# Sinkhorn attention and token/channel MLP on one core: first k mixing, q turns, k row tiles and the bf16 copies of u rearranged

## The chip, the core and the metric

The kernel runs on one core of one Trainium2 chip. The core has a matrix engine (TensorE, PE in the profile, with its weight loads as PEld), a vector engine (DVE), a scalar engine (ACT), GpSimd (POOL) and a sync engine (SP, which here only issues transfers); each takes its instructions in order. Matrix products read SBUF and write PSUM, which has eight banks; DVE and ACT bring results from PSUM to SBUF. The metric is the device time of one execution in microseconds (us).

## The reference, cut to what matters

```python
P = sort_net                                   # (4, 8, 8, 8): batch, head, block, block
for _ in range(5):
    P = exp(P - max(P, -1)); P /= sum(P, -1) + 1e-9; P /= sum(P, -2) + 1e-9
k_sorted = einsum('bhij,bhjcd->bhicd', P, k in 8 blocks of 96 tokens)
v_sorted = einsum('bhij,bhjcd->bhicd', P, v in 8 blocks of 96 tokens)
attn = softmax(0.125 * q_block @ k_sorted_block.T)      # within each block
x    = (attn @ v_sorted), heads side by side            # (4, 768, 512)
u    = x + lam * (w_tok @ (alpha1 * x + beta1))         # token mixing, w_tok 768 x 768
out  = u + lam * (relu((alpha2 * u + beta2) @ w_ch1) @ w_ch2)   # 512 -> 2048 -> 512
```

q, k and v have four batches, eight heads, 768 tokens and 64 columns. Everything comes in and goes out as float32; the products are made in float16 and bfloat16.

## The kernel before, in words

**The front (batch 0).** The five rounds of the softmax on `sort_net` run on DVE and ACT (L223 to L238); between ACT's exponential and DVE's next step, a list of small set-up operations (`side`, L192) is worked off two at a time. PE meanwhile runs `dense(14)`, products with the identity that nobody reads. `big_p(b)` (L251) spreads the 8x8 matrices of a batch into `PB[b]`, a block matrix of 128 rows. `k_group(b, g)` (L303) mixes the blocks of k, 32 small products of 32 rows in PSUM tile `psA` (two banks; two such tiles), emptied half by ACT and half by DVE into `kT`; six groups make a batch. In a group before the change, the rows used are two of the four 32-row strips of PE. `q_pair(b, p, pool, eng)` (L290) turns q of two heads by 12 transposes into one bank, and `eng` copies it to `qT`; the bank is from `psX`, which has a single buffer, or from `psM`, which has three. `v_first_layout` (L141) rearranges batch 0's v, in four parts, on POOL and ACT; `v_first` (L323) mixes it in eight groups. Then `score` (scores, and their maxima on DVE), `split_max` and `turn_max` (the maxima turned), `soft` (scores again minus the maximum, exponential on ACT) and `value` (weighted sum of v on PE, normalised by DVE into `x16`) are written out by hand from L560 to L632, between `w_tok_block` (the turn of w_tok) and `row_sums`.

**The rest.** Three things are generators that yield a cost after each piece, and `weave(main, other, ratio)` (L548) puts pieces of `other` between those of `main` as long as their cost stays under `ratio` times the cost of `main` so far. It so fixes the order of the instructions on every engine:

- `opening()`: token mixing of batch 0 (`token_mix`, L470: six tiles of 128 tokens, each six products of 512 columns, two or three DVE operations and a bf16 copy `u16` by ACT, L486), with the first four `u_turn` (L488: u turned on PE, ACT makes `a2T` of it) after four tiles. Woven with `ahead(1)` (L453): mixing of batch 1's v (`v_group`, then `v_relay`, a trip through DRAM), four `q_pair` on `psX` with ACT, six `k_group`.
- `both()`: `hidden(b, 0)` (16 groups of four products with W1), three `result` (16 products with W2, two DVE operations, a write of 256 KB), `hidden(b, 1)`; woven with `attention(b + 1)` (L434).
- `join()`: token mixing of batch b+1 with the three other results of batch b; woven with `ahead(b + 2)`.

The last batch has hidden and result alone. The order of transfers is that of the queues: POOL issues the loads of q, k, v, w_tok, W1 and W2, SP the small vectors, the relay of v and the results.

Of the kernel before, what the change touches and what calls it, by code (L numbers as in the profile page):

```python
# [19 lines left out]
def kernel(  # L20
# [20 lines left out]
    BLK = S // NB  # L41
# [105 lines left out]
    v_first_layout(1, G)  # L147
    v_first_layout(3, G)
    load_k(1)
    load_q(1)  # L150
# [14 lines left out]
    V.memset(v0T[:, BLK * D:], 0.0)  # L165
    ones_bf = wt([128, 1], BF, "ones_bf")
# [21 lines left out]
    def products():  # L188
        for n in range(2):
# [3 lines left out]
        lambda: V.tensor_copy(ident16[:], ident32[:]),  # L193
# [9 lines left out]
        lambda: V.tensor_reduce(  # L203
            m32[:], ident32[:].rearrange("p (g c) -> p c g", c=32), AXX, ALU.add
        ),
        lambda: V.tensor_scalar(nmask[:], m32[:], -1.0, None, op0=ALU.mult),
        lambda: make_sel(1),
        products,
# [5 lines left out]
    warm = bank(psM)  # L214

    def dense(n):
        for _ in range(n):
            PE.matmul(
                warm[:], identbf[:], identbf[:].unsqueeze(1).to_broadcast([128, 4, 128]),
                start=True, stop=True,  # L220
            )
# [3 lines left out]
    for it in range(5):  # L225
        A.activation(sortP[:], sortP[:], AF.Exp)
        for _ in range(2):
            side.pop(0)()
# [10 lines left out]
    dense(14)  # L239
# [6 lines left out]
    for n in range(2):  # L246
        SP.dma_start(vecs[n].rearrange("(c p) -> c p", p=128), va[:, n])
    SP.dma_start(a2col[:], moe_alpha2.rearrange("(c p) -> p c", p=128))
    SP.dma_start(b2col[:], moe_beta2.rearrange("(c p) -> p c", p=128))

# [39 lines left out]
    def q_pair(b, p, pool, eng):  # L290
        ps = bank(pool, F16)
        for kt in range(NT):
# [6 lines left out]
            eng, qT[b % 2][p][:, 0:S].rearrange("r (t k) -> r t k", k=NT),  # L299
            ps[:, 0:S].rearrange("r (k t) -> r t k", k=NT),  # L300
        )

    def k_group(b, g):  # L303
        raw, ps = rawk[b % 2], bankA()
        for turn in range(2):
            for tt in range(8):
                for hl in range(2):
                    bk = (hl + turn) % 2
                    th, tl = divmod(g * 16 + bk * 8 + tt, HALF)
                    r = slice(th * 64 + hl * 32, th * 64 + hl * 32 + 32)  # L310
                    PE.matmul(  # L311
                        ps[hl * 64:hl * 64 + 64, bk, tt * 32:(tt + 1) * 32],
# [4 lines left out]
        dst = kT[:, 0:H4 * S].rearrange("r (c t) -> r c t", t=BLK)  # L317
        dst = dst[:, :, g * 16:(g + 1) * 16].rearrange("r c (b t) -> r c b t", b=2)
        src = ps[:, :, 0:256].rearrange("r b (t c) -> r c b t", c=32)
# [114 lines left out]
    def attention(b):  # L434
        for p in range(H4):
            for g in range(2):
                score(b, p, g)
            yield 0.65
# [14 lines left out]
    def ahead(b):  # L453
# [6 lines left out]
        for p in range(H4):  # L460
            q_pair(b, p, psX, A)
            yield 0.4
# [7 lines left out]
    def token_mix(b, kt):  # L470
# [15 lines left out]
        A.copy(u16[:, kt], ub[:, kt])  # L486

    def u_turn(b, half, ci):  # L488
        ps = bank(psM, BF)
# [31 lines left out]

    def result(b, half, kk, turn=None):
        kt = half * 3 + kk
        ub = u[b]
# [23 lines left out]
    def weave(main, other, ratio):  # L548
        done = given = 0.0
        live = True  # L550
        for cost in main:
            done += cost
            while live and given < ratio * done:
# [6 lines left out]
    big_p(0)  # L560
    V.memset(mh[0][:], 0.0)
    for n in range(2):
        V.memset(ET[n][:, :, :, BLK:], 0.0)
    k_group(0, 0)
    k_group(0, 1)
    q_pair(0, 0, psM, V)
    k_group(0, 2)
    dense(1)
    q_pair(0, 1, psX, V)
    k_group(0, 3)  # L570
    dense(1)
    q_pair(0, 2, psM, V)
    k_group(0, 4)
    dense(1)
    q_pair(0, 3, psX, V)
    k_group(0, 5)
    dense(2)
    v_first_layout(0, A)
    v_first_layout(2, A)
    for g in range(2):  # L580
        score(0, 0, g)
    dense(2)
    for g in range(2):
        score(0, 1, g)
    dense(3)
    split_max(0, 0, 2)
    score(0, 2, 0)
    w_tok_block(0, A)
    turn_max(0)
    score(0, 2, 1)  # L590
    w_tok_block(1, A)
    v_first(0, V)
    v_first(1, A)
    for g in range(2):
        soft(0, 0, g)
    v_first(2, A)
    v_first(3, V)
    for g in range(2):
        score(0, 3, g)
    v_first(4, A)  # L600
    v_first(5, V)
    split_max(0, 2, 4)
    w_tok_block(2, A)
    for g in range(2):
        soft(0, 1, g)
# [99 lines left out]
```

## Time and profile before

| what | value |
|---|---|
| median of 3 runs | 339.48 us (338.79 to 341.17) |
| the profiled execution, its own time | 339.23 us |
| its span, first to last instruction | 337.1 us |
| mean granted clock of PE | 0.931 |
| PE busy, DVE busy, ACT busy, POOL busy | 300.1, 181.9, 137.9, 28.7 us |
| first small k product, first score, first value | 13.51, 24.88, 37.26 us |
| first token mixing, first hidden product | 50.97, 81.00 us |
| joins of batches 1, 2, 3 begin | 123.65, 197.70, 268.62 us |
| last product ends, last write issued | 332.4, 333.9 us |

A row of the windows gives the stretch in us, its length, and for each engine its busy time and number of instructions, then the granted clock of PE (1.00 is full), the share of the 16 transfer engines and GB/s. A row of waits names who waited for whom, the sum, how often and the longest. A row of the timeline gives start, duration, engine, line, operation, output and inputs, and in brackets the idle time ahead of it and what ended it. A group row gives line, engine, operation, shapes and count, then busy time and the mean ns of one. L numbers are those of the listing above.

### The profile page before, as it was taken

How to read it: one execution, taken by the hardware profiler on the slowest of the kernel's cores; microseconds unless marked ns; L12 is line 12 of the kernel's file. 1: busy time of each engine (PE TensorE's matmuls, PEld its weight loads, DVE VectorE, ACT ScalarE, POOL GpSimd, SP SyncE). 2: the span in 40 equal slices, each digit the busy share in tenths (PEclk: the TensorE clock that was granted, in tenths of full speed). 3: DMA queues.
4: the chain of work that ended last, by engine and by line, in shares of the span. 5: the costliest groups of instructions: out<-in, count | busy, mean ns of one | idle time of the engine just before them, and what ended most of it. 6: DMA issues, size and time to landing. Idle time of an engine off the chain costs nothing.

```text
span 337.1 us, 7773 instructions
## 1 busy us (share of the span) xinstructions
PE 300.1 (89%) x3453; PEld 170.7 (51%) x3453; DVE 181.9 (54%) x345; ACT 137.9 (41%) x242; POOL 28.7 (9%) x45
## 2 busy tenths in 40 slices
PE   5498768488999997998999996998999998899994
PEld 2365652254655653454655643555656644454641
DVE  6859646337914456277725364579344477413323
ACT  2129623344571535315651645245633413560510
POOL 7194230003000000000000000000000000000000
PEclk9658967778999999699999999999999999999998
DMA  7999999994901004900001007900001000001001
GB/s 126 209 231 205 212 202 210 257 130 71 204 3 64 33 0 120 103 33 31 2 2 64 33 1 135 110 9 31 2 33 64 1 33 31 31 2 62 31 33 63
DMA packets 33001, 27.13 MB, mean 80 GB/s; under 512 B 20724, under 2 KB 27656, under 8 KB 32904
## 3 DMA queue, kind: packets, MB, share of 16 engines
q0 software_dynamic: 8976, 14.81, 24.8%
q1 hardware_dynamic: 23992, 11.82, 17.4%
q8 instruction: 27, 0.44, 0.6%
q14 instruction: 6, 0.05, 0.0%
HBM read 32.79 MB, written 8.65 MB: 123 GB/s over the span
## 4 chain that ended last, share of the span: by engine, by line
PE 70%; DVE 19%; ACT 8%; issue 1%; POOL 0%; ACTq 0%; POOLq 0%
PE psM L507 23%; PE psM L527 23%; PE psM L479 6%; PE psA L420 4%; DVE u L485 3%; DVE tmix L484 3%; PE psA L311 3%; DVE u L474 2%; DVE tmix L536 2%; DVE u L537 2%; PE psA L392 2%; ACT u L486 2%; ACT u L137 2%; PE psA L343 2%; PE psA L363 2%
## 5 line engine op out<-in xcount | busy, mean ns | idle before, releaser
L507 PE MATMUL psM<-a2T,W 128*128 128x384 bf16 x512 | 91.2, 326 | 1.0 <-ACT hT L517 1.0
L527 PE MATMUL psM<-W,hT 128*128 128x512 bf16 x384 | 91.5, 386 | 0.0
L517 ACT ACTIVATE hT<-psM 128x384 bf16<-128x384 f32 x96 | 46.1, 490 | 54.1 <-PE psM L507 52.5
L507 PEld LDWEIGHTS <-W 128*128 128x128 bf16 x512 | 47.6, 98 | 31.6 <-issue 1.4
L527 PEld LDWEIGHTS <-hT 128*128 128x128 bf16 x384 | 36.0, 99 | 41.5 <-issue 4.4
L536 DVE TENSOR_TENSOR tmix<-psM,lamB 128x512 f32<-128x512 f32 x24 | 16.6, 691 | 51.6 <-PE psM L527 51.6
L486 ACT CAST u<-u 128x512 bf16<-128x512 f32 x24 | 14.8, 618 | 67.9 <-DVE u L485 67.9
L515 DVE TENSOR_SCALAR hT<-psM 128x384 bf16<-128x384 f32 x32 | 17.8, 556 | 43.5 <-PE psM L507 43.5
L479 PE MATMUL psM<-x,w_tokT 128*128 128x512 f16 x144 | 40.1, 427 | 0.2 <-ACT a2T L497 0.2
L404 ACT ACTIVATE ET<-psA 96x768 f16<-96x768 f32 x32 | 24.3, 804 | 24.9 <-PE psA L399 24.8
L368 DVE TENSOR_REDUCE mx<-psA 96x8 f32<-96x768 f32 x32 | 28.8, 946 | 0.9 <-PE psA L363 0.8
L484 DVE TENSOR_TENSOR tmix<-psM,a1lB 128x512 f32<-128x512 f32 x24 | 16.5, 686 | 14.1 <-PE psM L479 14.1
L479 PEld LDWEIGHTS <-w_tokT 128*128 128x128 bf16 x144 | 14.2, 105 | 18.4 <-issue 6.8
L497 ACT ACTIVATE a2T<-psM,b2col,a2col 128x384 bf16<-128x384 bf16 x32 | 20.6, 672 | 2.6 <-PE psM L491 2.6
L311 PEld LDWEIGHTS <-rawk 32*64 32x64 f16 x768 | 16.1, 123 | 9.1 <-issue 8.9
L311 PE MATMUL psA<-PB,rawk 32*64 32x32 f16 x768 | 17.4, 190 | 0.8 <-DVE PB L263 0.8
L474 DVE SCALAR_TENSOR_TENSOR u<-b1lB,rowsum,x 128x512 f32<-128x512 f32 x24 | 17.9, 744 | 0.0
L537 DVE TENSOR_TENSOR u<-u,tmix 128x512 f32<-128x512 f32 x24 | 16.6, 692 | 1.0
L485 DVE TENSOR_TENSOR u<-u,tmix 128x512 f32<-128x512 f32 x24 | 16.6, 692 | 0.8
L294 PE MATMUL psX<-ident,qn 128*64 128x128 f16 x168 | 8.3, 241 | 9.6 <-ACT qT L137 9.6
L320 ACT CAST kT<-psA 128x256 f16<-128x256 f32 x24 | 8.3, 373 | 20.1 <-PE psA L311 20.0
L321 DVE CAST kT<-psA 128x256 f16<-128x256 f32 x24 | 9.4, 418 | 12.8 <-ACT kT L320 12.8
(90 smaller groups left out, 266.3 us busy)
## 6 DMA issues: line engine op xcount, KB each, us to landing
out_dram<-u SPq DMA_DIRECT2D x24, 256.0 KB, 2.0
W<-in_moe_w_ch_dram POOLq DMA_DIRECT2D x8, 512.0 KB, 18.0
rawk<-in_k_dram POOLq DMA_DIRECT2D x8, 384.0 KB, 5.5
qn<-in_q_dram POOLq DMA_DIRECT2D x8, 384.0 KB, 7.9
rawv<-in_v_dram POOLq DMA_DIRECT2D x6, 384.0 KB, 11.1
vscr<-rawv SPq DMA_DIRECT2D x3, 768.0 KB
vS<-vscr SPq DMA_DIRECT2D x6, 384.0 KB
hT<-in_moe_w_tok_dram POOLq DMA_DIRECT2D x6, 192.0 KB, 12.5
```

Source lines behind the costliest of these rows:

```text
L311: PE.matmul(ps[hl * 64:hl * 64 + 64, bk, tt * 32:(tt + 1) * 32], raw[r, tl * D:(tl + 1) * D], PB[b][r, hl * H4:(hl + 1) * H4, :].rearrange ...
L368: V.tensor_reduce(mx[b % 2][:, :, c:c + 4], ps[0:BLK, :, 0:4 * BLK].rearrange("p l (i t) -> p l i t", t=BLK), AXX, ALU.max,)
L404: A.activation(ET[p % 2][:, :, g * 4:(g + 1) * 4, 0:BLK], ps[0:BLK, :, 0:4 * BLK].rearrange("p l (i t) -> p l i t", t=BLK), AF.Exp, scale= ...
L474: V.scalar_tensor_tensor(ub[:, kt], b1lB[:], rowsum[:, kt:kt + 1], x[:, kt], op0=ALU.mult, op1=ALU.add)
L479: PE.matmul(ps[:], w_tokT[:, ks, kt * 128:(kt + 1) * 128], x[:, ks, :], start=(ks == 0), stop=(ks == NT - 1),)
L484: V.tensor_tensor(t[:], ps[:], a1lB[:], ALU.mult)
L485: V.tensor_tensor(ub[:, kt], ub[:, kt], t[:], ALU.add)
L507: PE.matmul(ps[:, 0:TOK], W1[:, ci, m * 128:(m + 1) * 128], a2T_of[b, half, ci][:], start=(ci == 0), stop=(ci == CT - 1),)
L517: A.activation(t, ps[:, 0:TOK], AF.Relu)
L527: PE.matmul(ps[:], hT_of[m][:, kk * 128:(kk + 1) * 128], W2[:, m, :], start=(m == 0), stop=(m == HT - 1),)
L536: V.tensor_tensor(t[:], ps[:], lamB[:], ALU.mult)
L537: V.tensor_tensor(ub[:, kt], ub[:, kt], t[:], ALU.add)
```

## The change

What moves, in the order of the program:

- POOL issues `load_k(1)` ahead of v's layout and lays out three of v's four parts (before two); ACT has one part.
- One of two memsets of `ET` goes to the start, the other later. `side` has five operations, one in each round; the remaining masks, the selections of batches 1 to 3 and the products for the vectors become `more_masks()`, after the second k group. The writes of these vectors to DRAM (`vecs`) go behind the sixth k group.
- `dense` takes a bank of its own at each call; 22 in place of 14 run first, and 2, 3, 1, 1, 2 stand within the first k mixing (before 1, 1, 1, 2, and 2 and 3 between the scores).
- The first two q turns go ahead of the k groups, with ACT; groups 2 and 3 of batch 0's k are copied by DVE alone. The copy of a q turn takes its elements in another order: PSUM is read in sequence and `qT` is written in steps of six elements, before it was the other way round.
- `k_group` covers both halves of the tokens at once, so that its products use all four 32-row strips of PE in turn; `th` chooses the bank.
- In `ahead`, q is turned two pairs at a time into a `psA` tile, copied by ACT and DVE (`q_two`).
- `big_p` and the selections of later batches leave the stretch ahead of `opening`; `big_p(b + 1)` stands in `attention(b)`, which also yields 0.7 first. `row_sums` goes behind the third `value`. The weave of `opening` has ratio 0.9.
- `token_mix` no longer issues ACT's bf16 copy at once: it goes on a list `late` and is issued two pieces of `main` later (`tick`), or at the latest by the next `u_turn` that starts a half.
- The last tile's result of the last batch is made in two halves of 256 columns, each with its own write (`last_result`).

The diff, with most of the unchanged lines left out:

```diff
-    v_first_layout(1, G)
-    v_first_layout(3, G)
     load_k(1)
+    for part in range(1, 4):
+        v_first_layout(part, G)
     load_q(1)
...
     V.memset(v0T[:, BLK * D:], 0.0)
+    V.memset(ET[0][:, :, :, BLK:], 0.0)
     ones_bf = wt([128, 1], BF, "ones_bf")
...
     side = [
-        lambda: V.tensor_copy(ident16[:], ident32[:]),
         lambda: V.tensor_copy(identbf[:], ident32[:]),
...
         lambda: V.tensor_tensor(mask_h[:], m16[:, 0:8], m16[:, 8:16], ALU.add),
-        lambda: V.tensor_reduce(
-            m32[:], ident32[:].rearrange("p (g c) -> p c g", c=32), AXX, ALU.add
-        ),
-        lambda: V.tensor_scalar(nmask[:], m32[:], -1.0, None, op0=ALU.mult),
-        lambda: make_sel(1),
-        products,
     ]
...
     bc_j = [BH, NB, NB]
-    warm = bank(psM)
-
     def dense(n):
+        warm = bank(psM)
         for _ in range(n):
...
         A.activation(sortP[:], sortP[:], AF.Exp)
-        for _ in range(2):
-            side.pop(0)()
+        side.pop(0)()
+        if it == 0:
+            V.tensor_copy(ident16[:], ident32[:])
         V.tensor_reduce(srow[:], sortP[:], AXX, ALU.add)
...
     V.tensor_copy(P16[:], sortP[:])
-    dense(14)
+    dense(22)
...
     b1lB = wt([128, C], FT, "b1lB")
-    for n in range(2):
-        SP.dma_start(vecs[n].rearrange("(c p) -> c p", p=128), va[:, n])
+    V.tensor_reduce(m32[:], ident32[:].rearrange("p (g c) -> p c g", c=32), AXX, ALU.add)
     SP.dma_start(a2col[:], moe_alpha2.rearrange("(c p) -> p c", p=128))
     SP.dma_start(b2col[:], moe_beta2.rearrange("(c p) -> p c", p=128))
+
+    def more_masks():
+        V.tensor_scalar(nmask[:], m32[:], -1.0, None, op0=ALU.mult)
+        for b in range(1, B):
+            make_sel(b)
+        products()
...
     def q_pair(b, p, pool, eng):
-        ps = bank(pool, F16)
+        q_turn(b, p, bank(pool, F16), eng)
+
+    def q_turn(b, p, ps, eng):
         for kt in range(NT):
...
         copy(
-            eng, qT[b % 2][p][:, 0:S].rearrange("r (t k) -> r t k", k=NT),
-            ps[:, 0:S].rearrange("r (k t) -> r t k", k=NT),
-        )
-
-    def k_group(b, g):
+            eng, qT[b % 2][p][:, 0:S].rearrange("r (t k) -> r k t", k=NT),
+            ps[:, 0:S].rearrange("r (k t) -> r k t", k=NT),
+        )
+
+    def q_two(b, p):
+        ps = psA.tile([128, 2, 1024], F16, name="psA", tag="psA")
+        q_turn(b, p, ps[:, 0], A)
+        q_turn(b, p + 1, ps[:, 1], V)
+
+    def k_group(b, g, alone=None):
         raw, ps = rawk[b % 2], bankA()
-        for turn in range(2):
-            for tt in range(8):
-                for hl in range(2):
-                    bk = (hl + turn) % 2
-                    th, tl = divmod(g * 16 + bk * 8 + tt, HALF)
+        for tt in range(8):
+            for turn in range(2):
+                for th in range(2):
+                    hl = (th + turn) % 2
                     r = slice(th * 64 + hl * 32, th * 64 + hl * 32 + 32)
+                    tl = g * 8 + tt
                     PE.matmul(
-                        ps[hl * 64:hl * 64 + 64, bk, tt * 32:(tt + 1) * 32],
+                        ps[hl * 64:hl * 64 + 64, th, tt * 32:(tt + 1) * 32],
                         raw[r, tl * D:(tl + 1) * D],
...
                     )
-        dst = kT[:, 0:H4 * S].rearrange("r (c t) -> r c t", t=BLK)
-        dst = dst[:, :, g * 16:(g + 1) * 16].rearrange("r c (b t) -> r c b t", b=2)
-        src = ps[:, :, 0:256].rearrange("r b (t c) -> r c b t", c=32)
+        dst = kT[:, 0:H4 * S].rearrange("r (c h t) -> r c h t", h=2, t=HALF)
+        dst = dst[:, :, :, g * 8:(g + 1) * 8]
+        src = ps[:, :, 0:256].rearrange("r h (t c) -> r c h t", c=32)
+        if alone is not None:
+            copy(alone, dst, src)
+            return
         A.copy(dst[:, 0:16], src[:, 0:16])
...
     def attention(b):
+        yield 0.7
+        if b + 1 < B:
+            big_p(b + 1)
+            yield 0.1
         for p in range(H4):
...
         v_relay(b)
-        for p in range(H4):
-            q_pair(b, p, psX, A)
-            yield 0.4
+        for p in range(0, H4, 2):
+            q_two(b, p)
+            yield 0.8
         for g in range(0, 6, 2):
...
         V.tensor_tensor(ub[:, kt], ub[:, kt], t[:], ALU.add)
-        A.copy(u16[:, kt], ub[:, kt])
+        late.append([2, lambda: A.copy(u16[:, kt], ub[:, kt])])
+
+    late = []
+
+    def tick(all_of_them=False):
+        for item in list(late):
+            item[0] -= 1
+            if item[0] <= 0 or all_of_them:
+                late.remove(item)
+                item[1]()
     def u_turn(b, half, ci):
+        if half == 0 or ci == 0:
+            tick(True)
         ps = bank(psM, BF)
...
+    def last_result(b):
+        kt = NT - 1
+        for c in (slice(0, C // 2), slice(C // 2, C)):
+            ps = bank(psM)
+            for m in range(HT):
+                PE.matmul(
+                    ps[:, 0:C // 2], hT_of[m][:, 256:384], W2[:, m, c],
+                    start=(m == 0), stop=(m == HT - 1),
+                )
+            t = tmp([128, C], FT, "tmix", 3)
+            V.tensor_tensor(t[:, c], ps[:, 0:C // 2], lamB[:, c], ALU.mult)
+            V.tensor_tensor(u[b][:, kt, c], u[b][:, kt, c], t[:, c], ALU.add)
+            SP.dma_start(out[b, kt * 128:(kt + 1) * 128, c], u[b][:, kt, c])
+
     def result(b, half, kk, turn=None):
         kt = half * 3 + kk
+        if b == B - 1 and kt == NT - 1:
+            last_result(b)
+            return
         ub = u[b]
...
             done += cost
+            tick()
             while live and given < ratio * done:
...
     big_p(0)
+    q_pair(0, 0, psX, A)
+    q_pair(0, 1, psM, A)
+    k_group(0, 0)
+    dense(2)
+    k_group(0, 1)
+    v_first_layout(0, A)
+    more_masks()
     V.memset(mh[0][:], 0.0)
-    for n in range(2):
-        V.memset(ET[n][:, :, :, BLK:], 0.0)
-    k_group(0, 0)
-    k_group(0, 1)
-    q_pair(0, 0, psM, V)
-    k_group(0, 2)
+    V.memset(ET[1][:, :, :, BLK:], 0.0)
+    dense(3)
+    k_group(0, 2, V)
+    q_pair(0, 2, psX, V)
+    k_group(0, 3, V)
     dense(1)
-    q_pair(0, 1, psX, V)
-    k_group(0, 3)
-    dense(1)
-    q_pair(0, 2, psM, V)
+    q_pair(0, 3, psM, V)
     k_group(0, 4)
     dense(1)
-    q_pair(0, 3, psX, V)
     k_group(0, 5)
     dense(2)
-    v_first_layout(0, A)
-    v_first_layout(2, A)
+    for n in range(2):
+        SP.dma_start(vecs[n].rearrange("(c p) -> c p", p=128), va[:, n])
     for g in range(2):
         score(0, 0, g)
-    dense(2)
+    v_first(0, A)
+    v_first(1, A)
     for g in range(2):
         score(0, 1, g)
-    dense(3)
+    v_first(2, A)
+    w_tok_block(0, A)
     split_max(0, 0, 2)
     score(0, 2, 0)
-    w_tok_block(0, A)
+    w_tok_block(1, A)
     turn_max(0)
     score(0, 2, 1)
-    w_tok_block(1, A)
-    v_first(0, V)
-    v_first(1, A)
     for g in range(2):
         soft(0, 0, g)
-    v_first(2, A)
-    v_first(3, V)
+    v_first(3, A)
+    v_first(4, A)
     for g in range(2):
         score(0, 3, g)
-    v_first(4, A)
-    v_first(5, V)
+    v_first(5, A)
     split_max(0, 2, 4)
-    w_tok_block(2, A)
     for g in range(2):
         soft(0, 1, g)
+    w_tok_block(2, V)
+    turn_max(0)
     v_first(6, A)
     v_first(7, V)
-    turn_max(0)
+    value(0, 0)
     w_tok_block(3, V)
-    value(0, 0)
     for g in range(2):
         soft(0, 2, g)
-    w_tok_block(4, V)
     value(0, 1)
+    w_tok_block(4, A)
     for g in range(2):
...
     w_tok_block(5, A)
+    big_p(1)
+    value(0, 2)
     row_sums()
-    value(0, 2)
     SP.dma_start(a1lB[:], vecs[0].partition_broadcast(128))
...
     SP.dma_start(lamB[:], moe_lam.partition_broadcast(128))
-    big_p(1)
     value(0, 3)
...
     V.memset(mh[1][:], 0.0)
-    make_sel(2)
-    make_sel(3)
-    big_p(2)
-    big_p(3)
...
-    weave(opening(), ahead(1), 0.8)
+    weave(opening(), ahead(1), 0.9)
     for b in range(B):
```

## Prediction, made before the change had run

> **What bounds the kernel now.** I read the page's 40 slices first, then busy time in windows cut at the stages, then the waits of PE, then the order of time around the longest of them, and last the groups by form for prices. The row of granted clocks on the page:
>
> ```profile
> PEclk9658967778999999699999999999999999999998
> ```
>
> The steady part runs at full clock; digits 2 to 10 (8 to 84 us) do not, and one near 140 us does not. The windows by stage (busy time of PE, PEld, DVE, ACT, POOL with counts, granted clock, DMA share, GB/s):
>
> ```profile
> 12.50:24.90 12.40, 11.57 (x248) 8.49 (x249) 8.33 (x16) 2.74 (x7) 8.75 (x8) 0.50 1.13 218
> 24.90:37.30 12.40, 10.60 (x226) 7.51 (x226) 10.59 (x19) 11.98 (x13) 4.94 (x9) 0.89 1.12 207
> 37.30:51.00 13.70, 8.90 (x212) 7.77 (x212) 7.09 (x20) 3.91 (x5) 3.71 (x6) 0.77 1.13 206
> 51.00:82.00 31.00, 23.68 (x304) 11.48 (x303) 15.85 (x27) 11.72 (x20) 1.67 (x4) 0.77 1.06 171
> 123.70:155.70 32.00, 29.41 (x349) 14.49 (x348) 17.82 (x29) 12.31 (x21) 0.00 (x0) 0.89 0.46 67
> 197.70:226.60 28.90, 26.31 (x349) 13.30 (x347) 17.80 (x29) 12.31 (x21) 0.00 (x0) 1.00 0.51 74
> 226.60:268.60 42.00, 41.09 (x479) 24.91 (x478) 22.28 (x36) 20.01 (x37) 0.00 (x0) 1.00 0.07 27
> ```
>
> The stages are: first k mixing (PE, half clock); first scores to the first value (ACT busy 11.98 of 12.40); the other values (a chain, nobody full); the opening weave of batch 0's token mixing with batch 1's v, q and k (31.0 us with PE busy 23.7 at 0.77 clock); the joins of batches 1 and 2, the same 349 products in 32.0 and 28.9 us; and hidden layer with attention, where PE is full and only work removed counts. PE's waits after 50 us, in total, times, longest:
>
> ```profile
> PE psX L294 <- ACT qT L137: 9.6, 4, 2.5
> ...
> PE psA L363 <- DVE kT L321: 1.3, 1, 1.3
> PE psM L507 <- ACT hT L517: 1.0, 1, 1.0
> ```
>
> The first join in order of time shows why the q turn waits:
>
> ```profile
> 133.46 0.69 DVE L485 TENSOR_TENSOR u<-u,tmix 128x512 f32<-128x512 f32 x1
> 134.18 0.62 ACT L486 CAST u<-u 128x512 bf16<-128x512 f32 x1 [2.18 <-DVE u L485]
> 134.71 0.79 ACT L137 COPY qT<-psX 128x768 f16<-128x768 f16 x1
> 135.55 0.53 PE L294 MATMUL psX<-ident,qn 128*64 128x128 f16 x12 [2.53 <-ACT qT L137]
> ```
>
> ACT stands at the bf16 copy of u until DVE has made u; the copy of the q turn is behind it on ACT; psX has one buffer; PE is in order, so the next token mixing waits too. Clock changes lie on a grid of 3.41 us (down at 10.7, up at 27.7, down at 44.8, up at 55.1, down at 61.9, read from half-us windows): gaps of 2 to 3 us are what lowers the clock, and long 512-column products raise it; at 17 to 24 us PE is busy all the time with small k products and stays at half.
>
> **The change part by part.** The sum is made against the profiled execution, 339.23 us (span 337.1, 2.1 around it), 0.25 below the median of 339.48.
>
> *First k mixing, now 12.5 to 24.9.* 8 more dense products after the clock rose at 7.3 cost 8 x 0.22 and end near 10.2, before P is ready at 12.4: free. Two q turns now run while DVE makes PB (12.7 to 13.5); q's loads, issued by 4.5 with 7.9 to landing, are there. Then DVE and ACT decide, not PE. ACT: two q copies 2 x 0.80, k halves 2 x 0.37 to about 15.8, then one v layout 2.81 once v has landed (16.15). DVE from 15.4: two k halves 0.84, the masks, three selections and two products moved behind them (0.18 + 0.42 + 0.47, and they leave the softmax loop by about 0.2), two memsets 0.81 (the third sits in an idle gap before 2.3), two whole k copies at 0.68 (the 96x512 v row), two q copies at 0.96, two k halves 0.84: 6.8, so the first score at 22.2 to 22.8, against 24.87: -2.2. PE's own sum at half clock (4 x 0.78 of q, 6 x 0.96 of k, 9 x 0.43 dense = 12.7 from 12.9) would give 25.6, no gain; five dense products fall in the window 14.1 to 17.5 (2.1 of 3.4 us; 24.3 to 27.7 rose with 1.7 and the scores), so I take it that the clock rises at 17.5 or 20.9 and DVE decides.
>
> *Scores and values, 24.9 to 51.* ACT's two layouts (24.3 to 29.8) are replaced by one before the scores and a third on POOL, and PE is warm. The chain is then DVE: 8 maxima at 0.95, two splits, copies; I walk it to the first value at 34.2 (before 37.26: another -0.9 beside the 2.2). After it the alternation value 0.75, normalising 1.2, soft 0.4 stays; the row sums, which wait 1.1 for ACT and then take 1.0 ahead of the last two values, go behind value 2, and two `big_p` (1.6 of wait at 48.8 to 50.8) leave: -2.5. Together 50.97 becomes 45: **-6**, bounds -1 (clock stays down) and -8.
>
> POOL and SP: `load_k(1)`'s two issues (0.53 each) pass the layouts, from 21.6 to some 11 to 16, which fills the dip in DMA at 23.5; q, v and W issues come some 3 us later by the third layout (2.78). DMA stays full to 78 us either way; W arrives by about 55, needed at 66. On SP, the two small column loads go ahead of the vecs writes and these wait for DVE's products near 17; the broadcasts behind them took 6.9, needed at 45. The v relay starts some 8 us earlier into the same queue; even at its old end, 78, it is before value of batch 1, 16 us into the hidden layer. Free, with 4 us of cover.
>
> *Opening, 50.97 to first hidden product at 81.0: 30.0.* Removed: v's first copy no longer waits for u (55.1 against PE done at 54.4: 1.2), two q waits 2.4 + 2.1, and with the gaps the half clock of 61.9 to 65.3 and 68.7 to 72.1 (3.4 of 6.8). q in twos adds DVE 2 x 0.96. Walked from the first mixing's start, its first 2.7 at half clock and the rest warm: v 0 to 2 end at 5.1 (the third waits for the first one's copy, 1.0), mixing 1 to 6.4, q in twos to 8.5, mixing 2 to 9.8, two k groups to 11.0, mixing 3 to 12.3, two k groups to 13.4 (one waits for DVE's half). Then the four a2T, where the flush puts the copy of tile 3 ahead of them on ACT as before: u of tile 3 ends at 14.8 on DVE, the copy at 15.4, the first a2T at 16.0. PE stands some 2.5 there, which is what is late next. Mixings 4 and 5 and two k groups end at 20.4; with one more cold window 21: **-9**, bounds -5 and -10.5.
>
> *Joins.* Two waits of 2.5, and 3.1 by which the first is longer than the second for its half clock at 137 to 143. q's second copy stands on DVE behind a u of 0.69 and holds psA for the second k group: some 0.4 each. **-7.2**, bounds -4 and -8.1. The third join has no q: 0.
>
> *Entry to the hidden layer.* Attention yields first, so DVE finishes tile 5 before the first maxima: 1.3 + 0.9 + 0.9 of waits, and 1.0 in the last batch, where ACT's copy stood ahead of three hT. Attention ends 1.9 us of PE later; the last value then has 1.95 of PE work behind it and needs 1.3. **-3**, bounds -1 and -4.1.
>
> *k in four row tiles.* 64 products took 1.11 warm (17 ns each), 1.89 cold. Halved, six pairs in the joins save 6 x 0.55 = 3.3; if issue is the floor, 0. The ratio 1.7 of cold to warm says array, mostly, but 17 ns is the shortest spacing in this trace: **-1.2**. *Tail.* Two half results: DVE after PE 0.84 (512 columns 0.69, with about 0.15 fixed) for 1.40, and a smaller last write: **-0.7**, bounds -0.4 and -1.2.
>
> *The q copy* now reads in order and stores 12 bytes apart. Below: 0.56, the unit-step w_tok copy on DVE; above: the layout's rate.
>
> ```profile
> L137 ACT COPY u<-u 64x1536 f16<-64x1536 f16 x2 | 5.5, 2810 | 0.0
> ...
> L139 DVE COPY qT<-psX 128x768 f16<-128x768 f16 x2 | 1.9, 958 | 1.0 <-PE psX L294 1.0
> ```
>
> 2810 / 1536 = 1.83 ns an element, 1.41 for 768. I take the old 0.80 and 0.96, the nearest shape: 0, up to +3. The Trainium skill (SBUF — State Buffer, Door 1: The DMA port swizzle) says that a 16-byte line must be hit twice to run at full rate, which 12-byte steps mostly miss; no row here stores so, the layout reads 128 bytes apart at half rate, which agrees, and by the rule the sum would be 315.
>
> Sum: -6 - 9 - 7.2 - 3 - 1.2 - 0.7 = -27.1: **312**. The good ends, -35.2, give 304; the poor ends, -11.4, with the +3 of the q copy give 331.
>
> **The rivals.** *Slow q stores* (1.41 a copy): DVE +0.9 in the front, some 1 in the opening, 0.5 in each of two joins: +3, 315. *The clock stays low* in front and opening: for it, PE was full at 14 to 24 and stayed at half; against, the dense products. Front -2, opening -4 (DVE's waits go, the slow products stay), joins -5, entry -3, tail -0.7: -14.7, 324.5. *No change*: the gains of front, opening, joins and k all turn into waits for DVE, which is in order and takes on two q copies a batch; half the entry and the tail stay: -1.5 - 0.7, 337. Against it, DVE is busy 15.9 of 31.0 and 17.8 of 28.9 there. *The other side: four row tiles run one at a time.* One k product takes 178 ns from start to end; pairs of tiles overlap now. The new order writes bank 0 from two row tiles and bank 1 from two. Should each wait for the one before: 768 x (178 - 17) = 124 us, 436. It decides from 35 ns more per product (27 / 768). Against it: two row tiles with 64 of the columns each already overlap at 17 ns. The Trainium skill (TensorEngine Tiling (Array Packing), Gotcha 1: PSUM Pressure) says that different row tiles cannot access one PSUM bank at a time; the old order kept each pair in different banks and no run here shows the other; by it the k term falls to 0 at least, 313.
>
> **How the numbers follow.** Forecast 0.54, own range 305 to 319; slow stores 0.14; low clock 0.22; no change 0.04; other side 0.06. The range 304 to 326 leaves out the last two and tails of the others, some 0.2. A measurement tells about 1% from no change. Faster by over 1%: 0.54 + 0.14 + 0.22 = 0.90; within: 0.04; slower: 0.06.
>
> **What would show it.** Granted clock 1 by 21 us; first score near 22.5; first token mixing near 45; first hidden product near 66; no PE wait on qT above 0.5; both joins 26 us, no half clock near 140; 64 k products under 1.1; ACT's q copy at 0.80. Wrong if a new wait on psA or kT above 1 us stands in the joins, if DVE fills the opening, or if k products space out beyond 50 ns.

## The result, and the profile after

The changed kernel takes 348.53 us (median of 4 runs, 347.85 to 349.09) against 339.43 of the kernel before in the same comparison (4 runs, 338.79 to 341.17): a ratio of 1.0259, 95% interval 1.0217 to 1.0301 (the pairs in brackets behind later ratios are such intervals too). It is slower by 2.6%, where 312 was forecast. Some kernels have runs over 1.5% above their fastest; medians and ratios below leave those out. The profiled execution took 347.85, span 345.7, against 339.23 and 337.1: +8.6.

The row of granted clocks after:

```profile
PEclk9865696867899999999999998999999999999999
```

The half clock near 140 us is gone, as forecast. From 8 to 84 us digits below 9 still stand among the others. The stages, in windows cut at the same events as before (columns as in the prediction):

```profile
12.50:34.50 22.00, 9.99 (x251) 5.68 (x252) 15.83 (x19) 9.23 (x7) 15.49 (x15) 0.60 0.97 177
...
57.40:88.10 30.70, 21.87 (x304) 10.28 (x304) 20.07 (x27) 14.51 (x19) 3.19 (x6) 0.72 0.99 151
...
129.20:161.40 32.20, 24.68 (x347) 12.14 (x348) 22.47 (x31) 14.83 (x20) 0.00 (x0) 1.00 0.45 67
```

The first k mixing grew from 12.4 to 22.0 us, with PE busy for only 9.99 of them; it had been busy for 11.57 of 12.4. The opening kept its length (31.0 before, cut alike). The first join has the full clock and 4.7 us less PE work than before (24.68 against 29.41), and is no shorter (32.2 against 32.0): what the clock gave went into waits. Who waits for whom, PE only (lines of the changed kernel: L295 the transposes of q, L317 the k products, L137 and L139 the copy helper for ACT and DVE, L515 and L521 the turn of u and its copy):

```profile
PE psA L295 <- ACT qT L137: 16.8, 6, 2.8
PE psA L317 <- DVE kT L139: 8.0, 2, 6.1
...
PE psM L515 <- ACT a2T L521: 3.2, 4, 1.6
...
PE psA L317 <- DVE qT L139: 2.2, 2, 1.1
```

The wait for q's copy grew from 9.6 to 16.8, though the copy no longer stands behind u. The groups by form say what the copy costs now (L245 makes `nmask`, the first of the masks):

```profile
L139 DVE COPY qT<-psA 128x768 f16<-128x768 f16 x6 | 16.3, 2718 | 16.6 <-PE psA L295 16.5
L137 ACT COPY qT<-psA 128x768 f16<-128x768 f16 x6 | 16.2, 2708 | 10.2 <-PE psA L295 10.2
...
L245 DVE TENSOR_SCALAR nmask<-m 128x32 bf16<-128x32 f32 x1 | 6.3, 6350 | 0.0
```

2.7 us a copy, where the old order of the elements took 0.80 on ACT and 0.96 on DVE. With the four of the front that is 16 copies. And an operation of 32 columns takes 6.35. The first join in order of time, rows of q alone:

```profile
135.53 2.70 ACT L137 COPY qT<-psA 128x768 f16<-128x768 f16 x1 [0.41 <-PE psA L295]
...
138.28 0.53 PE L295 MATMUL psA<-ident,qn 128*64 128x128 f16 x12 [2.80 <-ACT qT L137]
...
144.34 0.53 PE L295 MATMUL psA<-ident,qn 128*64 128x128 f16 x12 [2.81 <-ACT qT L137]
```

The second turn of `q_two` writes the other bank, but of the same tile, and starts only when ACT has emptied the first. PE, in order, stands 2.8 us each time, six times in all. The front, rows of ACT, DVE and POOL put in order of time:

```profile
13.65 2.71 ACT L137 COPY qT<-psX 128x768 f16<-128x768 f16 x1 [3.15 <-PE psX L295]
15.98 2.96 ACT L137 COPY qT<-psM 128x768 f16<-128x768 f16 x1
17.95 8.21 POOL L139 COPY u<-u 64x1536 f16<-64x1536 f16 x3
18.55 0.87 ACT L329 CAST kT<-psA 128x256 f16<-128x256 f32 x2
19.19 0.76 DVE L330 CAST kT<-psA 128x256 f16<-128x256 f32 x2 [5.99 <-ACT kT L329]
19.86 6.35 DVE L245 TENSOR_SCALAR nmask<-m 128x32 bf16<-128x32 f32 x1
```

ACT's two q copies hold it until 18.55, its halves of `kT` come after them, DVE's halves after those, and so DVE reaches `nmask` at 19.86, when POOL has begun v's three layouts. `nmask` ends at 26.21, 0.05 after the last of them. A later k group waits 6.1 for a `kT` copy that stands behind it on DVE.

From these I formed two theories. A: the new order of the elements alone makes the kernel slow, by the copy's own time and by what it delays. B: the wait of the masks is a second, separate cause, and the rest of the change brings what was forecast less what the clock withholds.

### The profile page after: what moved, and what is told of

It is laid out like the page before. It is cut to its first block, busy times and chain, and to the rows that moved or that the text cites. A ratio compares the mean times of both kernels' runs of the same rounds, so it can differ in the third digit from the quotient of the medians.

```text
span 345.7 us, 7807 instructions
## 1 busy us (share of the span) xinstructions
PE 291.9 (84%) x3457; PEld 166.4 (48%) x3476; DVE 202.0 (58%) x348; ACT 149.8 (43%) x238; POOL 31.4 (9%) x46
## 3 DMA queue, kind: packets, MB, share of 16 engines
q0 software_dynamic: 8976, 14.81, 24.1%
## 4 chain that ended last, share of the span: by engine, by line
PE 67%; DVE 14%; ACT 8%; DMA 7%; issue 2%; POOL 1%; DVEq 0%; POOLq 0%; ACTq 0%
PE psM L531 24%; PE psM L568 21%; PE psM L492 6%; ACT qT L137 5%; PE psA L429 3%; DVE qT L139 3%; DMA vscr<-rawv 3%; DMA qn<-in_q_dram 3%; PE psA L372 2%; DVE mx L377 2%; PE psA L401 2%; DVE nmask L245 2%; DMA vS<-vscr 2%; PE psA L352 1%; PE psA L408 1%
## 5 line engine op out<-in xcount | busy, mean ns | idle before, releaser
L568 PE MATMUL psM<-W,hT 128*128 128x512 bf16 x349 | 84.1, 382 | 2.1 <-issue 1.6
L568 PEld LDWEIGHTS <-hT 128*128 128x128 bf16 x368 | 33.8, 98 | 38.4 <-issue 2.4
L577 DVE TENSOR_TENSOR tmix<-psM,lamB 128x512 f32<-128x512 f32 x23 | 16.1, 701 | 43.6 <-PE psM L568 43.6
L492 PE MATMUL psM<-x,w_tokT 128*128 128x512 f16 x144 | 39.0, 416 | 1.6 <-DVE x L437 1.3
L139 DVE COPY qT<-psA 128x768 f16<-128x768 f16 x6 | 16.3, 2718 | 16.6 <-PE psA L295 16.5
L521 ACT ACTIVATE a2T<-psM,b2col,a2col 128x384 bf16<-128x384 bf16 x32 | 20.4, 667 | 4.4 <-PE psM L515 4.4
L317 PE MATMUL psA<-PB,rawk 32*64 32x32 f16 x768 | 10.9, 190 | 13.2 <-DVE kT L139 8.0
L295 PE MATMUL psA<-ident,qn 128*64 128x128 f16 x144 | 6.8, 236 | 16.8 <-ACT qT L137 16.8
L137 ACT COPY qT<-psA 128x768 f16<-128x768 f16 x6 | 16.2, 2708 | 10.2 <-PE psA L295 10.2
L317 PEld LDWEIGHTS <-rawk 32*64 32x64 f16 x768 | 9.5, 121 | 20.3 <-issue 20.1
L295 PEld LDWEIGHTS <-qn 128*64 128x64 f16 x192 | 6.9, 119 | 23.1 <-issue 22.4
(100 smaller groups left out, 318.5 us busy)
## 6 DMA issues: line engine op xcount, KB each, us to landing
rawv<-in_v_dram POOLq DMA_DIRECT2D x6, 384.0 KB, 10.6
```

Source lines behind the costliest of these rows:

```text
L137: A.copy(dst, src)
L139: eng.tensor_copy(dst, src)
L317: PE.matmul(ps[hl * 64:hl * 64 + 64, th, tt * 32:(tt + 1) * 32], raw[r, tl * D:(tl + 1) * D], PB[b][r, hl * H4:(hl + 1) * H4, :].rearrange ...
L492: PE.matmul(ps[:], w_tokT[:, ks, kt * 128:(kt + 1) * 128], x[:, ks, :], start=(ks == 0), stop=(ks == NT - 1),)
L521: A.activation(t[:], ps[:, 0:TOK], AF.Identity, bias=b2col[:, ci:ci + 1], scale=a2col[:, ci:ci + 1])
L568: PE.matmul(ps[:], hT_of[m][:, kk * 128:(kk + 1) * 128], W2[:, m, :], start=(m == 0), stop=(m == HT - 1),)
```

## The experiments

**The old order of elements, all else changed** (e1_q_old):

```diff
-            eng, qT[b % 2][p][:, 0:S].rearrange("r (t k) -> r k t", k=NT),
-            ps[:, 0:S].rearrange("r (k t) -> r k t", k=NT),
+            eng, qT[b % 2][p][:, 0:S].rearrange("r (t k) -> r t k", k=NT),
+            ps[:, 0:S].rearrange("r (k t) -> r t k", k=NT),
```

> The changed kernel with the q copy's old order alone (PSUM read in steps, qT stored in sequence). Theory S (the stores in steps of 12 bytes make all 16 q copies 2.7 us, and PE waits behind them): copies back to 0.80 on ACT and 0.96 on DVE; PE's waits for q copies (16.8 in 6) fall to about 5 in 6; each join 32.4 to about 27.5, opening 29.8 to about 24, front 3 earlier; about 329. Theory M (what made it slower is DVE held at nmask while POOL lays out v, 6 us at 20 to 26): little changes in time, 343 to 347, since the front is still held. Rival R (the order of the work, not the price of a copy): 346 or more.

319.94 us (319.05 to 320.75), ratio to before 0.9463 (0.9361 to 0.9565). These two lines cost 348.53 - 319.94 = 28.6 us. The expected 329 was 9 too high: it had counted 3 in the front, where the first token mixing comes some 10 earlier (47.5 in place of 57.4). The copies took 0.80 and 0.96 again, and `nmask`, which this kernel reaches before POOL begins its layouts at 17.6, took 0.17:

```profile
15.79 0.17 DVE L245 TENSOR_SCALAR nmask<-m 128x32 bf16<-128x32 f32 x1
```

**The masks right behind `big_p(0)`** (e2_masks_early, the new order kept) **and both edits** (e3_both).

```diff
     big_p(0)
+    more_masks()
     q_pair(0, 0, psX, A)
...
     v_first_layout(0, A)
-    more_masks()
```

> The changed kernel with the masks, selections and vector products (more_masks) issued right after PB, ahead of the time POOL lays out v. Theory M: nmask back from 6.35 to 0.18, first token mixing some 6 earlier (57.4 to about 51.5), about 342.5. Theory S with M as a second part: the same 342 to 343, the joins unchanged at 32. If S were all: no change, 348.

342.23 us (341.1 to 345.42), 1.0129 (1.001 to 1.0247): -6.3 against the changed kernel; `nmask` took 0.18 at 13.1.

> Both edits together. S and M as two separate causes: the savings add, first token mixing at 45 to 47, first hidden product at 68 to 70, total 320 to 325. If a third cause holds the kernel (R): above 330.

318.53 us (314.85 to 319.22, 3 of 4 runs), 0.9384 (0.9236 to 0.9531). The savings do not add: 28.6 and 6.3 apart, 30.0 together. Theory B fell in its first half. DVE is late for the masks only because ACT's q copies make it late, so the wait belongs to the one cause. The next two runs try theory A from the other side.

**The new order alone, in the kernel before** (e5_before_q_steps).

```diff
-            eng, qT[b % 2][p][:, 0:S].rearrange("r (t k) -> r t k", k=NT),
-            ps[:, 0:S].rearrange("r (k t) -> r t k", k=NT),
+            eng, qT[b % 2][p][:, 0:S].rearrange("r (t k) -> r k t", k=NT),
+            ps[:, 0:S].rearrange("r (k t) -> r k t", k=NT),
```

> The kernel before with the new q copy alone (PSUM read in sequence, qT stored in steps of 12 bytes). Theory S: each of 16 copies goes from 0.80 or 0.96 to 2.7; four stand in the front on DVE (DVE's round of 1.8 becomes 3.5 against PE's 2.28: about 1.2 x 4 = 5 more), twelve with ACT on the single psX buffer (some 1.9 each on PE's path, less where products cover it: 12 to 20); 356 to 365. Rival (copies become slow only beside other work of the changed kernel, such as both engines storing at once): copies near 1, 340.

360.66 us (359.75 to 361.81) against 337.67, 1.0654 (1.056 to 1.0748): +23.0. ACT's copy took 2709 ns and DVE's 2759, and PE's wait for it went from 9.6 to 20.2:

```profile
PE psX L294 <- ACT qT L137: 20.2, 8, 4.3
```

**The old order for batch 0 only** (e15_front_old: `q_two` still stores in steps).

```diff
-    def q_turn(b, p, ps, eng):
+    def q_turn(b, p, ps, eng, steps=False):
...
+        o = "r (t k) -> r k t" if steps else "r (t k) -> r t k"
+        i = "r (k t) -> r k t" if steps else "r (k t) -> r t k"
...
-        q_turn(b, p, ps[:, 0], A)
-        q_turn(b, p + 1, ps[:, 1], V)
+        q_turn(b, p, ps[:, 0], A, True)
+        q_turn(b, p + 1, ps[:, 1], V, True)
```

> The changed kernel with the q copy's old order for batch 0 (front) alone; the twelve copies in q_two still store in steps. If the front holds 10 to 13 of the loss as the profiles of the changed kernel and of the one with old copies say (first token mixing at 57.4 and 47.5 or 44.5): first mixing at 45 to 48, opening still near 30, joins still 31 to 32, total 336 to 339, no change against before. Rival (the front's loss is given back later, covered by the opening): 344 or more.

337.55 us (5 of 10 runs; all lie between 335.25 and 347.52) against 338.80 (11 of 13 runs), 0.9986 (0.9939 to 1.0033): no change against before. So the loss of 28.6 splits into some 11 in the front, with the wait of the masks (348.53 - 337.55), and some 17.6 in the opening and the joins (337.55 - 319.94). The profiles agree for the front: the first token mixing starts at 46.8 here, 10.6 earlier than in the changed kernel. The opening took 26.9, not the expected 30, and the joins 35.4 (granted clock 0.86) and 32.4 (full clock).

**What holds `nmask`** (e13_layout_act: all four of v's layouts on ACT, none on POOL).

```diff
-    for part in range(1, 4):
-        v_first_layout(part, G)
...
-    v_first_layout(0, A)
+    for part in range(4):
+        v_first_layout(part, A)
```

> The changed kernel with all four parts of v's layout on ACT, none on POOL. Theory M (nmask on DVE waits for POOL's copies and for nothing else): nmask near 0.18 though it stands at the same place behind the two k groups; first k mixing then ends where ACT lets it (four layouts of 2.8 behind the q copies). Rival (nmask waits for a tile or a semaphore of its own): again 5 us or more, whatever POOL does. The time is no verdict, ACT has 8 us more in the front.

```profile
19.50 0.17 DVE L243 TENSOR_SCALAR nmask<-m 128x32 bf16<-128x32 f32 x1
```

The same place, the q copies still slow, and 0.17 in place of 6.35: it was POOL's copies that held it. The Trainium skill (SBUF — State Buffer, Who interferes with whom) says that DVE and GpSimd share one pair of ports, that a copy or `tensor_scalar` can take it in a two-port mode, and that whoever comes second is blocked entirely. These two traces agree: blocked through to the end of POOL's third copy, and not slowed when there was none. Which mode `nmask` ran in, the traces do not show. Not every operation of DVE is held: the two `kT` copies at 19.19, which read PSUM, ran beside POOL's first copy at some 0.4 each. (Whole kernel 345.08, one run.)

**The price of a store in steps** (e9_probe: the kernel before, and behind its end copies of one 768-column PSUM tile, float16 stored singly in steps of 1 to 16 elements by ACT and DVE in turn, then 512 columns as float32; its whole time is compared with nothing).

```diff
+    for step in (1, 2, 3, 4, 6, 8, 12, 16):
+        for eng in (A, V):
+            copy(
+                eng, qT[0][0][:, 0:S].rearrange("r (t k) -> r k t", k=step),
+                ps[:, 0, 0:S].rearrange("r (k t) -> r k t", k=step),
+            )
```

> The kernel before with 22 copies added behind its end, the output as before: 768 float16 elements from PSUM into qT in steps of 1, 2, 3, 4, 6, 8, 12 and 16 elements, and 512 into float32 in steps of 2, 4 and 8, each on ACT and on DVE. Theory L (a price for each store that leaves a small line): duration grows with the step up to some step and is flat from there, float32 steps of 4 as dear as float16 steps of 8. Theory W (a price for a store narrower than 4 bytes that its neighbour does not follow): a jump from step 1 to step 2 and flat behind it, float32 without a jump. Both: 2.7 at step 6.

ACT's copies in steps of 1, 3, 4, 6, 8 and 16, then float32 ones in steps of 2 and 8:

```profile
334.99 0.80 ACT L137 COPY qT<-psA 128x768 f16<-128x768 f16 x1 [10.93 <-PE psA L679]
...
338.53 1.43 ACT L137 COPY qT<-psA 128x768 f16<-128x768 f16 x1 [1.07 <-DVE qT L139]
...
341.46 1.86 ACT L137 COPY qT<-psA 128x768 f16<-128x768 f16 x1 [1.50 <-DVE qT L139]
...
345.24 2.70 ACT L137 COPY qT<-psA 128x768 f16<-128x768 f16 x1 [1.92 <-DVE qT L139]
...
350.71 3.55 ACT L137 COPY qT<-psA 128x768 f16<-128x768 f16 x1 [2.77 <-DVE qT L139]
...
364.98 3.36 ACT L137 COPY qT<-psA 128x768 f16<-128x768 f16 x1 [3.58 <-DVE qT L139]
...
371.77 0.61 ACT L137 CAST tmix<-psA 128x512 f32<-128x512 f16 x1 [3.43 <-DVE qT L139]
...
375.31 1.07 ACT L137 CAST tmix<-psA 128x512 f32<-128x512 f16 x1 [1.12 <-DVE tmix L139]
```

DVE took the same as ACT but for step 1 (0.55). With 1.01 at step 2 and 1.86 at step 4, all steps from 2 to 8 fit 0.17 + 768 x 0.55 ns x step: the cost goes by the bytes that the stores pass over, 4.4 ns for each 16, up to one store in 16 bytes, and no further (3.52 at 12, 3.36 at 16). The kernel's step of six is this row: 2.70. Float32 stores of 512 columns cost 1.05 at step 4 and 1.07 at step 8, that is (1.05 - 0.17) / 512 = 1.7 ns each; at step 2, two to 16 bytes, they cost 0.61 on ACT and 0.69 on DVE. So the duration has the shape that theory L gives, up to 16 bytes and then flat, but float32 is cheaper, as theory W has it.

**Is it the step or the half word?** (e12_probe2: as above, with two or four float16 neighbours stored together, then reads in steps.)

```diff
+    for w, step in ((2, 2), (2, 4), (4, 2), (2, 8), (4, 4)):
+        for eng in (A, V):
+            copy(
+                eng, qT[0][0][:, 0:S].rearrange("r (t k w) -> r k t w", k=step, w=w),
+                ps[:, 0, 0:S].rearrange("r (k t w) -> r k t w", k=step, w=w),
+            )
```

> The kernel before with copies added behind its end, the output as before: float16 stores of two or four neighbours at a time, in steps of 8 to 32 bytes; single float16 stores in steps of 4, 6 and 8 elements again; and contiguous stores of what is read from SBUF in steps of 2 to 16 elements. The first probe gave 4.4 ns for each 16 bytes passed by single float16 stores and 1.7 by float32 ones. Theory W (halves of a 4-byte word are dear): stores of two neighbours in 16-byte steps cost 1.7 to 2 ns a pair, like float32. Theory L (any line visited costs 4.4 ns in a float16 tensor): 4.4 a pair, 384 pairs 1.8 us. Reading in steps: the v layout read 128 bytes apart at 1.83 ns an element; about 1.4 to 1.6 us for 768 at step 8 and 16.

Pairs 16 bytes apart, ACT and DVE (32 bytes apart both took 0.84, and 8 bytes apart ACT 0.80 and DVE 0.55, as in sequence):

```profile
336.97 0.83 ACT L137 COPY qT<-psA 128x768 f16<-128x768 f16 x1 [0.66 <-DVE qT L139]
337.83 0.83 DVE L139 COPY qT<-psA 128x768 f16<-128x768 f16 x1 [0.90 <-ACT qT L137]
```

DVE's row shows the price, since ACT's 0.83 is hardly above its 0.80 in sequence: 384 pairs cost what 384 float32 cost, (0.83 - 0.17) / 384 = 1.7 ns each; the singles 16 bytes apart cost 4.4. It is single float16 stores, half of a 4-byte word each, that are dear, and more so the more bytes they pass over, up to 16; 4-byte stores cost the same at 16 and 32 bytes, and less at 8. The item that was to repeat the single stores in steps of 4, 6 and 8 did something else: it read PSUM in steps of 192, 128 and 96 elements and stored in sequence, which took 0.80 on ACT and 0.96 on DVE at all three. That is the old order's price: reading PSUM in steps costs ACT nothing, and DVE 0.41. Reading SBUF in steps, stores in sequence, took ACT 0.83, 0.86, 1.20, 1.54 and 1.56 at 2, 4, 6, 8 and 16 elements.

**Two good parts alone, in the kernel before.** Four row tiles for k (e6_before_k4; `dst` and `src` follow, as in the change):

```diff
-        for turn in range(2):
-            for tt in range(8):
-                for hl in range(2):
-                    bk = (hl + turn) % 2
+        for tt in range(8):
+            for turn in range(2):
+                for th in range(2):
+                    hl = (th + turn) % 2
...
-                        ps[hl * 64:hl * 64 + 64, bk, tt * 32:(tt + 1) * 32],
+                        ps[hl * 64:hl * 64 + 64, th, tt * 32:(tt + 1) * 32],
```

> The kernel before with k mixed in four row tiles alone. Theory K (tiles overlap four at a time): 64 products at full clock 1.11 to 0.68 as in the changed kernel, the first stage shorter by up to 2 before DVE binds it, two groups' 0.43 in 6 places of the joins: 3 to 5 less, about 335. Rival (the k products are covered by copies everywhere): within 1 of before.

334.52 us (332.45 to 335.2) against 337.67, 0.9887 (0.9785 to 0.9989). One group of 64 products in the joins, first the kernel before, then the changed one (0.68 in e6_before_k4 too):

```profile
145.21 1.09 PE L311 MATMUL psA<-PB,rawk 32*64 32x32 f16 x64
```

```profile
154.98 0.68 PE L317 MATMUL psA<-PB,rawk 32*64 32x32 f16 x64
```

Row tiles that share a bank, each writing its own half of the partitions, do overlap: 10.6 ns a product, in place of 17. The late copies of u (e7_before_late; `tick` as in the change, in `weave` and in `u_turn`):

```diff
-        A.copy(u16[:, kt], ub[:, kt])
+        late.append([2, lambda: A.copy(u16[:, kt], ub[:, kt])])
```

> The kernel before with the late bf16 copies of u alone. Theory: ACT no longer stands at u, PE's waits for the q copy in opening and joins (9.6 in 4) fall to what psX with one buffer leaves (under 1 each), the first join loses its half clock: 8 to 14 less, about 328. Rival (the wait goes to psX with the next copy, or u's copy is late for the turn of u): 335 or more.

325.46 us (324.55 to 326.32), 0.9612 (0.9527 to 0.9698). The wait for q fell from 9.6 to 3.6, the opening from 30 to 24.1, the joins (first token mixing to first hidden product) from 32.2 and 29.1 to 27.2 each, and the half clock near 140 went. This one edit is most of what the change has to give.

**From the old order to a better kernel.** Each of these has both edits of e3_both and those of the ones told before it. Both turns of `q_two` ahead of both copies (e4_both_two_first):

```diff
-        q_turn(b, p, ps[:, 0], A)
-        q_turn(b, p + 1, ps[:, 1], V)
+        q_products(b, p, ps[:, 0])
+        q_products(b, p + 1, ps[:, 1])
+        q_copy(b, p, ps[:, 0], A)
+        q_copy(b, p + 1, ps[:, 1], V)
```

> Both edits, and in q_two the 24 products of both turns are issued ahead of the two copies. Theory T (the second turn's products wait for the copy of the first turn because both banks are one tile): PE's waits for q copies in q_two, about 0.85 each in 6 places, go to near 0; 3 to 4 less than the kernel with both edits, about 318. Rival (these waits are covered, or return as a wait for the DVE copy): within 1 of it.

316.01 us (313.67 to 316.47), 0.9325 (0.923 to 0.9419). PE's wait for ACT's copy inside the pair (5.3 in 6 in e1_q_old and e3_both) is gone, and half of it comes back one step later: the k products wait 2.8 in 3 for DVE's copy, behind a u on DVE. A flush of only those copies of u that the next turn reads was meant to follow (e10_flush; `below` replaces `all_of_them`):

```diff
-            if item[0] <= 0 or all_of_them:
+            if item[0] <= 0 or item[2] < below:
...
-        if half == 0 or ci == 0:
-            tick(True)
+        if ci == 0:
+            tick((half + 1) * 3)
```

> The kernel with old q copy, early masks and both turns' products first, and in addition the flush ahead of the turn of u issues only the bf16 copies of the tiles that this turn reads (three of the first half, then the rest). Theory F: in the opening ACT no longer stands at tile 3 ahead of four a2T, PE's waits there (3.2 in 4) fall to about 1, two less in time, and 0.5 less at each of the later first turns: about 313. Rival (the wait goes to the turns' own chain, or DVE is the bound there): within 1 of 316.

314.46 us (313.5 to 317.41), 0.9296 (0.9228 to 0.9363). But the flush still counted down the others, so every engine got its instructions in the same order as in e4_both_two_first, and the wait for `a2T` stayed 3.2. It is a repeat: 316.01 and 314.46 show what one program spreads. Both q copies on ACT (e11_q_act, on top of e10_flush):

```diff
-        q_copy(b, p + 1, ps[:, 1], V)
+        q_copy(b, p + 1, ps[:, 1], A)
```

> As the one before, with both q copies of q_two on ACT (0.80 each) in place of one on DVE. Theory: PE's waits of k products for a q copy on DVE (2.8 in 3) go, DVE is freer by 0.96 twice a batch; 1 to 3 less. Rival (ACT's copies of k and v come later by as much): within 1.

311.08 us (309.5 to 312.33), 0.9166 (0.9098 to 0.9233); the k products' wait fell from 2.8 to 0.6. Then the flush so that it counts nothing down (e14_flush_fewer):

```diff
-            item[0] -= 1
+            item[0] -= 0 if below else 1
             if item[0] <= 0 or item[2] < below:
```

> The kernel with old q copy, early masks, both turns' products first and both q copies on ACT, in which the turn of u now really issues the copies of only those tiles that it reads: in the opening ACT makes the first a2T ahead of the copy of tile 3. Theory F: PE's waits for a2T (3.2 in 4) fall to 2 or less, the opening is some 1 shorter; 309 to 310.5 against 311.1. Rival (DVE's u of tiles 3 to 5 bounds the opening): 311 within the spread of 1.5.

309.11 us (307.73 to 310.28) against 338.80 of before (11 of 13 runs), 0.9115 (0.9055 to 0.9175): better than both kernels by 30 and 39 us. What is left of the waits for `a2T` (L500 the token mixing, L523 the turn of u in this kernel):

```profile
PE psM L500 <- ACT a2T L529: 1.1, 2, 0.9
PE psM L523 <- ACT a2T L529: 0.6, 2, 0.4
```

The opening is 17.9 us here, from 20.6 in e11_q_act, but the granted clock in it was 1.00 here and 0.84 there, and the runs of the two kernels overlap (307.73 to 310.28, 309.50 to 312.33). The shorter waits are shown; what they are worth in time is not.

## Why the prediction was wrong, point by point

**The step that failed: "I take the old 0.80 and 0.96, the nearest shape: 0, up to +3."** Measured: 2.7 us a copy, and +28.6 for the kernel. The sum of all 16 copies is 43.6 us after and 14.0 in e1_q_old, so 29.6 us of ACT and DVE came in, and the time grew by nearly as much, since q's copy stands where PE waits for it and DVE's lateness met POOL. Three things went wrong in the step. The upper bound, 1.41, was the price of another thing: the layout *reads* SBUF in steps and stores in sequence; a row with stores in steps did not exist, and a bound should then have been left open instead of being closed by the nearest read. The follow-on was priced at one copy's extra time on DVE (0.9 in the front, 0.5 in a join), though in `q_two` both turns share a tile, so the second turn waits for the first copy: six times 2.8. And DVE's lateness was priced as lateness alone, not as a meeting with POOL, which cost another 6.2. The rival "slow q stores" named the mechanism; its 315 had the wrong price. The Trainium skill (SBUF — State Buffer, Door 1: The DMA port swizzle) puts the penalty at fewer than two hits on a 16-byte line. The traces agree for 4-byte stores: 512 float32 took 0.61 on ACT with two in 16 bytes and 1.05 with one. Single float16 stores are slow before that: DVE took 1.01 for 0.55 at step 2, with four in 16 bytes, and ACT 1.86 for 0.80 at step 4, with two. At 1.7 ns a store, 768 stores would take some 1.5 us; the kernel paid 2.7, and the rest is the half word's.

**The other terms**, read from e3_both (the change without its two slow causes) against before, profiled execution against profiled execution: front -6.4 (forecast -6; first score 22.1, first token mixing 44.5), opening -8.0 (forecast -9), joins with k -6.8 (forecast -7.2 and -1.2), entry to the hidden layer -2.25 (forecast -3), tail -0.9 (forecast -0.7). The sum is -24.4, against -27.1 with q at nothing. (That execution is 3.7 below e3_both's median, so by medians the change without its slow copies gives less, 318.5 to 319.9; the forecast was still some 7 too low there.) In the changed kernel itself the parts gave, against before: front +6.5, opening -0.3, joins +4.8, entry -1.45, tail -0.9, together +8.6.

**Entry.** The 1.0 of the last batch did not come: from its sixth token mixing to the last product it is 45.06 us before and after. The wait for hT did go, and in the changed kernel the turn of u waits as long for the copy of u that was put back:

```profile
303.39 0.23 PE L515 MATMUL psM<-identbf,u 128*128 128x128 bf16 x1 [0.98 <-ACT u L499]
```

**Joins.** 27.2 each in e3_both and e7_before_late, where 26 was forecast, counted like the 32.0 and 28.9 of before. What the forecast had missed inside them is the wait within `q_two`, 0.9 a time and two in a join even with the old order (5.3 in six).

**The k row tiles.** The rival of tiles one at a time fell (0.68 for 64, where it needed 11). As work of PE the term of 1.2 was too small: of at most 0.55 a pair, 0.41 was reached, 2.5 in the six pairs. e6_before_k4 gained 3.2 by the medians, with an interval of 0.4 to 7.3, but little of it in the joins as such: in its profile the second join, at full clock in both kernels, went from 29.1 to 28.6. More came in the front (first token mixing 2.2 earlier) and in the first join (32.2 to 28.6), which lost its half clock.

**The clock.** Neither the forecast (full by 21 us) nor the rival "clock stays low" describes it. Rows of e1_q_old and then e3_both, which differ by the place of six small DVE steps:

```profile
PEclk9975596979999999999999999999999999999999
```

```profile
PEclk9956988979999999999999999999999999999999
```

From 22 to 35 us the granted clock was 0.50 in the one and 0.76 in the other. Runs of one kernel also differ in it: e3_both spreads over 5.6 us. The dense products do not decide it alone. What in the front tips a window I have not settled; it is worth some 3 us and hides differences of that size between kernels.

**Not settled.** Why a store of half a word costs 4.4 ns and pairs 1.7 is measured and not explained. The 12.9 us that the changed kernel's front lost against e3_both is measured by e15_front_old only as a whole (some 11 by medians); the copies' own part and the blocked `nmask`, 6.2 in the profile, were not taken apart further than e2_masks_early's 6.3.

## What to carry to other kernels

Store 16-bit results in sequence, or at least in pairs, and let the read from PSUM take the steps: here that is 0.80 for 2.7 us, and a copy that PE waits for passes most of its price on: of 30.2 us that the 16 copies grew by in e5_before_q_steps, 23.0 came through. A bound for an operation that no row shows must come from the same kind of access (store or read, element size); a row that only looks alike is no bound. Before an engine is made late, look at what it will then run beside: a step that DVE ran in 0.17 us took 6.35 beside POOL's copies.

## What the runs showed of the hardware that was not expected

- Single float16 stores to SBUF in steps of 2 to 8 elements took 0.17 us + 0.55 ns x step for each element on 128 partitions, the same on ACT and DVE; pairs (on DVE) and float32 (on both) took about 1.7 ns a store at steps of 16 and 32 bytes, and less at 8.
- ACT read PSUM in steps of 96 to 192 float16 elements at the price of reading in sequence (0.80 for 768); DVE went from 0.55 to 0.96.
- A DVE operation of 0.17 us was held for 6.35 by three GpSimd copies in a row, through both of their seams.
- Four 32-row tiles, two to a bank, ran at 10.6 ns a product of 32 columns, two tiles at 17.
